# Batch 0's scores computed with tokens on partitions, and x of the other batches loaded without states

## Chip, cores and metric

One core of one Trainium2 chip. The metric is device time in microseconds of one execution. The kernel before: median 666.43 us of three runs (665.96 to 667.14). Its profiled execution took 665.46 us, 663.3 of them from the first instruction to the last.

## What is computed

For each of 8 batches and 8 heads, 512 tokens `x` and 32 states `state` of 64 numbers attend to each other, and the result, 544 rows of 512 numbers a batch, goes through a gated layer:

```python
scores  = scale * x @ state.T          # 512 x 32, softmax over the states
xread   = softmax(scores)  @ state     # 512 rows out
scores2 = scale * state @ x.T          # 32 x 512, softmax over the tokens
sread   = softmax(scores2) @ x         # 32 rows out
h = concat(xread, sread) reshaped to 4352 x 512
out = ((h @ w_a) * (h @ w_b)) @ w_out  # d_ff = 1536
```

## The kernel before

**Stages.** The program is recorded first and ordered afterwards. `Recorder` (L195 on) collects units: one instruction, or several under `rec.together`. `plan` (L699) works out from given costs when each unit is due (`late`), adds to that the table `SHIFTS` (L316) and gives each unit an earliest time from the table `RELEASES` (L530), both by a running number of groups of units; then it fills the engines' queues in time. Within an engine the order is fixed by this; SP issues all DMAs in one order. All instructions are issued by one loop, so the profile puts nearly all of them down to L1798, and one goes by the tiles' names.

**Order of the work.** `VISITS` (L33) lets each batch pass through the d_ff chunks 0 and 1 of 6 (of 256 columns), then the other chunks are worked batch by batch (`SEVEN`, `FOUR`, L35), at last the 256 state rows. Ahead of a batch's first products stands `attend(b)` (L1617); the weights are brought in and split by `open_chunk` (L1674), `Conv` and `Whole` (L917, L960). TensorE works with pairs of tiles `_h` and `_l`: a number is split into a high part and a rest, and a product is three products of parts.

**Batch 0's way to its first product.** `Attention.load` (L1100) loads x transposed: for a pair of heads, features on 128 partitions (two heads of 64), 512 tokens in the free dimension, two such pairs for each of two groups `g`. The host appends to each of these 512 columns 64 of the states, padded: the first head's 32 states stand in the first 64 rows and 32 columns, the second head's in the other rows and columns, and zeros elsewhere. So a row of x is 576 numbers, `self.x` its first 512 and `self.st` the rest. The tile `x` has one buffer. Of batch 0, group 0 comes in two loads, one for each half `h`; all other groups come in one.

`scores(g)` (L1111) multiplies float32 states (64x32) by x (512 columns), four products for a group, each into 32 rows of a PSUM tile `ms`. So states are on partitions, heads in the order of `place_of` (L992). `copied(g)` (L1128) brings that into one half of `p_raw` on ScalarE, `store` (L1135) writes it to DRAM (`kept`) for the softmax over tokens, which comes in `read(b)` (L1653) much later.

The softmax over states needs states in the free dimension. A batch in `WIDE` (L51), that is batch 0 alone, gets there by TensorE: `scores_t` (L1138) transposes the four blocks of 128 tokens into an `acc` tile (`acc<-ident,p_raw` in the profile). `soft_t` (L1146) takes the maximum over 32 states and subtracts it on VectorE; `exp` (L1192) is ScalarE's; `norm` (L1195) is sum, +1e-9, reciprocal and product on VectorE; `back_t` (L1154) transposes back on TensorE (`acc<-ident,s_p`) and splits the result into high and low part with help of a product by -1 (`parts_of`, L898: `sd_h`, `sd_l` are batch 0's two tiles). The other batches go through `turn` and `back` (L1184, L1204), where VectorE transposes 32x32 blocks itself, and their `scores` are made for both groups at once.

For the first products (`ab<-sd_h,p_h` and the like, `product`, L1419) the weights' share for a batch is made by `direct` (L1298): states on 64 rows from `states_raw` (L1061, tile `xst`, all batches' states, loaded in four pieces), times converted weights `wo`. `states_raw` is loaded for batches 0 to 3 first and for 4 to 7 not before 50 us in the plan's time.

**Filling.** Before there is work, TensorE multiplies a tile `y` by itself, `WARM` = 80 times (L892 to L896), into a tile that nothing reads. The order of these among other units is the plan's.

**The end.** The last state rows leave through `layer2` (L1457): for the last 128 rows the two halves of 256 columns are multiplied, added and stored one after the other, columns 256 to 511 first (L1468).

Of the kernel before, what the change touches and what calls it, by code (L numbers as in the profile page):

```python
# [295 lines left out]
class Engine:  # L296
# [20 lines left out]
    0: 961, 1: 522, 2: -345, 3: -1004, 4: 175, 5: 340, 6: 86993674, 7: 86992534, 8: -40, 9: 377, 10: -272, 11:  # L317
    -285, 12: 1910712395119901894770688, 13: -228, 14: 836668491679242834149376, 15: -10, 16: 1824, 17: -285,
    18: -10666, 20: 605, 21: -1033, 22: 528, 23: 107510836717052703539200, 24: 539, 25: 53223186493590233677824,
    26: -1380, 27: 130, 28: -254, 29: 177, 30: -397, 31: 21675430, 32: -630, 33: 783445305185652701134848, 34:  # L320
    -951, 35: -13, 36: -642, 37: -5155, 38: 36215977, 39: -877, 40: 48965331574103428038656, 41: 42, 42: -635,
    43: -1228, 44: -269, 45: 2071, 46: -472, 47: -577, 48: 102188518067693636550656, 49: -9, 50: 676, 51: 520,
    52: 719217, 53: 33, 54: 714, 55: 53223186493590233677824, 56: -11, 57: 13732, 58: 517, 59: -2841, 60: 177,
    61: -972, 62: -23, 63: -53223186493590208512000, 64: 873, 65: 818137, 66: -164, 67: -474, 68: 604052, 69:
    -208, 70: 817687, 71: 2541, 72: -322, 73: 1208, 74: 707126, 75: -2962, 76: 593704, 77: -285, 78: -413, 79:
    369, 80: 593791, 82: -710700, 83: -27, 84: -173, 85: 110582, 86: -140, 87: 240, 88: 125076, 89: 85, 90:
    1396, 91: 32, 92: 6008, 93: 407, 94: -1248, 95: -79, 96: -1909, 97: -119, 98: 383, 99: -172095, 100: 629,
    101: -276, 102: -439, 103: -61, 104: -8159, 105: -1335, 106: 102, 107: 179, 108: -391, 109: -217, 110: 190,
    111: -26, 112: 6, 113: 64, 114: -1302, 115: 76, 116: 150039, 117: -631, 118: 183174, 119: -7, 120: 611, 121:
    225, 122: -3461, 123: -347, 124: -31117, 125: -316, 126: -250, 127: -119, 128: 662, 129: 197, 130: 291, 131:  # L330
    -53, 132: 476, 133: -1773, 134: 979, 135: 496, 136: -53223186493590208512000, 137: -619, 138: 5, 139: 448,
    140: 161, 141: 208554, 142: -104, 143: 1036873, 144: 784, 145: -43, 146: -759, 147: 635, 148: -24167, 149:
    795, 150: -2348, 152: 18204, 154: -118, 155: 1344, 156: -1474, 157: 78, 158: 2092, 159: -1478, 160: -272,
    161: -418, 162: -31, 163: -417, 164: -25074, 165: -2, 166: 17936, 167: -71, 168: -7661, 169: -270, 170:
    -18782, 171: 213, 172: 216, 173: -1, 174: -716, 175: -1464, 176: 691, 177: -323, 178: -579, 179: -194, 180:
    50, 181: 59, 182: -276, 183: -464, 184: -69, 186: 18395, 187: 122, 188: -49252, 189: 484, 190: 1157, 191:
    1278, 192: -12766, 193: 1667, 194: -127, 195: -358, 196: 3208, 197: 52, 198: 33, 199: -563, 200: -301, 201:
    109, 202: -119779, 203: 119, 204: -25, 205: -454, 206: 20, 207: -5082, 208: -388458, 209: 581, 210: -6, 211:
    -2508, 212: 471, 213: 316, 214: -242, 215: 1314, 216: -1260, 217: -731, 218: 306, 219: 1, 220: -120, 221:
    1068, 222: -8035, 223: -1303, 224: -20681, 225: 925, 226: 38867, 227: -408, 228: -232, 229: -10521, 230:  # L340
    330, 231: -11913, 232: 60, 233: 391, 234: -7142, 236: 3392, 237: -2739, 238: -903, 239: 305, 240: -163, 241:
    -688, 242: 303, 243: -2430, 244: -1182, 245: 137, 246: 104, 247: -610, 248: -102, 249: -208, 250: 196, 251:
    16, 252: 650, 254: -101, 255: -62, 256: 73, 257: -98, 258: 602, 259: 110, 260: 4, 261: 184, 262: -43, 263:
    -114, 264: -270, 265: 379, 266: 2005, 267: -144, 268: 305, 269: 172, 270: 1565, 271: 262, 272: -266, 273:
    1021, 274: 389, 275: 215, 276: 3038, 277: 233, 278: 665, 279: -618, 280: -2599, 281: 2762, 282: -483, 283:
    -652, 284: -429, 285: -17, 286: -7023, 287: -1082, 288: -25, 289: -694, 290: -10, 291: 1559, 292: 2347, 293:
    1599, 294: 145, 295: 347, 296: 700, 297: -436, 298: 555, 299: 1336, 300: -46, 301: 677, 302: 494, 303: -188,
    304: -614, 305: -1829, 306: 332, 307: 178, 308: -480, 309: -933, 310: 131, 311: -747, 312: -496, 313: -423,
    314: 219, 315: -289, 316: -421, 317: 28, 318: 904, 319: -283, 320: -309, 321: -429, 322: -381, 323: 651,
    324: 1261, 325: -662, 326: 12, 327: -714, 328: 132, 329: -520, 330: 718, 331: -1558, 332: 112, 333: -554,  # L350
    334: -354, 335: -772, 336: 429, 337: 112, 338: -755, 339: -867, 340: -2, 341: 654, 342: -385, 343: 2716,
    344: -754, 345: 801, 346: 60, 347: 1152, 348: 1039, 349: 137, 350: 2270, 351: 1354, 352: 296, 353: 226, 354:
# [1488 lines left out]
```

## Time and profile before

| what | value |
|---|---|
| median of three runs | 666.43 us |
| profiled execution, whole | 665.46 us |
| its span, first to last instruction | 663.3 us |
| PE busy | 654.2 us (99%) |
| DVE busy | 548.8 us (83%) |
| ACT busy | 383.0 us (58%) |
| moved by DMA | 155.98 MB, mean 235 GB/s |
| chain that ended last | PE 93%, DVE 5%, issue 1% |

PE is TensorE's products, PEld its weight loads, DVE VectorE, ACT ScalarE, SP the engine whose queue issues the DMAs. A busy PE counts the modelled ends of pipelined products, so that neighbouring ones overlap. A row of the timeline merges neighbours of one kind: `x8` are eight of them, the length is from the start of the first to the end of the last. Names are written out<-in with buffer numbers left out. In square brackets stands the idle time of the engine before the row and what ended it.

### The profile page before, as it was taken

How to read it: one execution, taken by the hardware profiler on the slowest of the kernel's cores; microseconds unless marked ns; L12 is line 12 of the kernel's file. 1: busy time of each engine (PE TensorE's matmuls, PEld its weight loads, DVE VectorE, ACT ScalarE, POOL GpSimd, SP SyncE). 2: the span in 40 equal slices, each digit the busy share in tenths (PEclk: the TensorE clock that was granted, in tenths of full speed). 3: DMA queues.
4: the chain of work that ended last, by engine and by line, in shares of the span. 5: the costliest groups of instructions: out<-in, count | busy, mean ns of one | idle time of the engine just before them, and what ended most of it. 6: DMA issues, size and time to landing. Idle time of an engine off the chain costs nothing.

```text
span 663.3 us, 12126 instructions
## 1 busy us (share of the span) xinstructions
PE 654.2 (99%) x4451; PEld 546.1 (82%) x4451; DVE 548.8 (83%) x1219; ACT 383.0 (58%) x707; POOL 0.7 (0%) x6
## 2 busy tenths in 40 slices
PE   7999999999999999999999999999999999999997
PEld 5566776776777778888888989898989989889996
DVE  5999989998877787878989978877777879877885
ACT  4677478699989976654545543534444444424442
POOL 0000000000000000000000000000000000000000
PEclk9999999999999999999999999999999999999999
DMA  8998579899989999866767764754426217168830
GB/s 304 354 366 332 222 253 344 301 317 356 351 300 393 339 327 351 328 189 198 257 235 219 246 232 124 249 168 159 155 101 169 102 48 223 65 182 188 233 97 33
DMA packets 75450, 155.98 MB, mean 235 GB/s; under 512 B 7040, under 2 KB 26240, under 8 KB 75392
## 3 DMA queue, kind: packets, MB, share of 16 engines
q1 hardware_dynamic: 75392, 155.22, 69.9%
q8 instruction: 35, 0.57, 0.4%
q14 instruction: 23, 0.19, 0.1%
HBM read 92.27 MB, written 62.91 MB: 234 GB/s over the span
## 4 chain that ended last, share of the span: by engine, by line
PE 93%; DVE 5%; issue 1%; DMA 0%; ACT 0%; DVEq 0%
PE ab L1798 44%; PE acc L1798 39%; PE ms L1798 10%; DVE t L1798 1%; DVE wo L1798 1%; DVE m L1798 1%; DVE s_p L1798 1%; DMA x<-xt 0%; DVE stg L1798 0%; DVE p_l L1798 0%; DVE x L1798 0%; ACT p_h L1798 0%; DVE a_sb L1798 0%; DVE u_c L1798 0%; DVE wq L1798 0%
## 5 line engine op out<-in xcount | busy, mean ns | idle before, releaser
L1798 PE MATMUL acc<-wo,g_h 128*128 128x256 f32 (+1 forms) x868 | 178.8, 316 | 0.3 <-DVE stg L1798 0.2
L1798 PEld LDWEIGHTS acc<-wo,g_h 128*128 128x128 f32 x868 | 135.4, 190 | 19.5 <-issue 3.4
L1798 PE MATMUL ab<-at_l,p_h 128*128 128x512 f32 x368 | 144.5, 393 | 0.0
L1798 PE MATMUL ab<-at_h,p_h 128*128 128x512 f32 x368 | 144.4, 397 | 0.0
L1798 PE MATMUL ab<-at_h,p_l 128*128 128x512 f32 x368 | 143.1, 391 | 0.0
L1798 PE MATMUL acc<-wo,g_l 128*128 128x256 f32 (+1 forms) x587 | 127.3, 308 | 0.2
L1798 PEld LDWEIGHTS acc<-wo,g_l 128*128 128x128 f32 x587 | 93.0, 190 | 11.5 <-issue 1.2
L1798 ACT CAST g_h<-a_sb 128x512 fp32r<-128x512 f32 (+1 forms) x104 | 64.0, 615 | 56.3 <-DVE a_sb L1798 26.6
L1798 PEld LDWEIGHTS ab<-at_h,p_h 128*128 128x128 f32 x368 | 69.1, 188 | 17.5 <-issue 2.9
L1798 PEld LDWEIGHTS ab<-at_h,p_l 128*128 128x128 f32 x368 | 69.1, 188 | 15.5 <-issue 0.8
L1798 PEld LDWEIGHTS ab<-at_l,p_h 128*128 128x128 f32 x368 | 69.3, 188 | 12.1 <-issue 0.8
L1798 DVE TENSOR_TENSOR g_h<-a_sb,g_h 128x512 fp32r<-128x512 f32 x68 | 46.7, 686 | 15.6 <-PE acc L1798 11.7
L1798 ACT COPY wq<-ab 128x512 f32<-128x512 f32 (+1 forms) x48 | 27.3, 569 | 43.5 <-PE ab L1798 43.3
L1798 DVE TENSOR_TENSOR wq<-ab,wq 128x512 f32<-128x512 f32 (+1 forms) x48 | 32.0, 666 | 21.9 <-PE ab L1798 18.9
L1798 ACT CAST p_h<-p_raw 128x1024 fp32r<-128x1024 f32 x32 | 33.7, 1054 | 21.7 <-PE ab L1798 20.5
L1798 DVE TENSOR_TENSOR p_l<-p_raw,p_h 128x1024 fp32r<-128x1024 f32 x32 | 39.0, 1218 | 1.5 <-ACT p_h L1798 1.4
L1798 DVE TENSOR_TENSOR stg<-acc,stg 128x256 f32<-128x256 f32 (+1 forms) x68 | 36.4, 552 | 3.6 <-PE acc L1798 2.6
L1798 ACT CAST g_l<-wq 128x384 fp32r<-128x384 f32 x46 | 23.6, 515 | 27.1 <-PE acc L1798 24.4
L1798 DVE TENSOR_TENSOR g_l<-wq,g_l 128x384 fp32r<-128x384 f32 x46 | 25.5, 555 | 14.5 <-PE acc L1798 9.8
L1798 ACT COPY p_raw<-ms 128x512 f32<-128x512 f32 x48 | 27.6, 591 | 10.7 <-PE ms L1798 8.5
L1798 DVE TENSOR_SCALAR t<-t 128x512 int32<-128x512 int32 x64 | 26.8, 420 | 5.3 <-ACT t L1798 5.0
L1798 DVE TENSOR_TENSOR a_sb<-ab,a_sb 128x512 f32<-128x512 f32 (+1 forms) x36 | 23.6, 657 | 6.7 <-PE ab L1798 5.3
(135 smaller groups left out, 1065.3 us busy)
## 6 DMA issues: line engine op xcount, KB each, us to landing
p_raw<-scr SPq DMA_DIRECT2D x32, 512.0 KB, 4.8
raw<-wl SPq DMA_DIRECT2D x20, 512.0 KB, 5.6
x<-xt SPq DMA_DIRECT2D x15, 576.0 KB, 7.1
out<-stg SPq DMA_DIRECT2D x33, 256.0 KB, 2.3
su<-wq SPq DMA_DIRECT2D x16, 512.0 KB, 5.8
scr<-sw_st SPq DMA_DIRECT2D x32, 256.0 KB, 4.6
scr<-p_raw SPq DMA_DIRECT2D x32, 256.0 KB, 4.8
x<-xn SPq DMA_DIRECT2D x16, 512.0 KB, 5.1
```

The source lines that it names most:

```text
L1798: getattr(obj, method)(*map(real, args), **{k: real(x) for k, x in kw.items()})
```

## The change

For batch 0, `scores_t` no longer transposes scores: it computes them again in the layout that it needs. Blocks of 128 tokens of x are the weights (128 rows, both heads), the 64 padded state columns are what is streamed, and the product lands with tokens on partitions. That is eight products a group. In this layout group 1's heads stand in another order than `place_of` has it, so its subtraction is done in two halves that put the columns right. The row scores of batch 0 (states on partitions) are made after that for both groups in one set; their copies and stores follow. The extra cost that the plan adds to the first scores (600) goes over to group 0's `scores_t`.

Batches 1 to 7 take their states for the row scores from `states_raw`, and their x is loaded without the 64 padded columns of each row (512 numbers in two runs for a partition, in place of one run with both rows and paddings). The tile `p_raw` is taken at the scores instead of at the first copy. At the end, the two halves of the last 128 rows change places. Both tables of the plan are replaced as a whole, so the order of instructions on all engines is a new one; of their some 730 changed lines the first of each stand here.

```diff
@@ -314,372 +314,377 @@
 
 
 SHIFTS = {
...
-    0: 961, 1: 522, 2: -345, 3: -1004, 4: 175, 5: 340, 6: 86993674, 7: 86992534, 8: -40, 9: 377, 10: -272, 11:
...
+    1: -301, 2: 282, 3: -635, 4: -579, 5: 1064, 6: 306437818579271978743496704, 8: -142422053665657027033038848,
...
 }
 
 RELEASES = {
...
-    0: 72, 1: 82, 2: 106, 5: 521, 6: 18, 8: 43, 9: 53, 10: 80, 13: 117, 14: 129, 19: 101, 20: 121, 21: 141, 23:
...
+    0: 12, 1: 115, 2: 125, 4: 495, 5: 531, 6: 56, 7: 55, 8: 61, 9: 89, 11: 130, 14: 187, 15: 191, 18: 187, 19:
...
 }
 
 
@@ -1105,29 +1110,28 @@
                     for h in range(2):
                         nc.sync.dma_start(out=x[:, g, h], in_=xt[self.b, g, :, h])
                 else:
-                    u = nc.sync.dma_start(out=x[:, g], in_=xt[self.b, g])
+                    w = S + D if self.wide else S
+                    u = nc.sync.dma_start(out=x[:, g, :, :w], in_=xt[self.b, g, :, :, :w])
                     u.rel = max(0, self.b - 3) * LATER / 2
 
         def scores(self, *gs):
 
             for g in gs:
                 self.s[g] = ps_ms.tile([P, 512], F32, name="ms")
-            with rec.together() as u:
+            self.pair = mlp.tile([P, NG, S], F32, name="p_raw")
+            with rec.together(self.pair) as u:
                 for hq in range(4):
                     for g in gs:
                         hh, j = hq % 2, place_of(g, hq)
                         rows = slice(hh * D, (hh + 1) * D)
                         nc.tensor.matmul(self.s[g][j * NS:(j + 1) * NS],
-                                         lhsT=self.st[rows, g, hq // 2, hh * NS:(hh + 1) * NS],
+                                         lhsT=self.st[rows, g, hq // 2, hh * NS:(hh + 1) * NS] if self.wide else
+                                         states_raw[rows, 2 * g + hq // 2, self.b * NS:(self.b + 1) * NS],
                                          rhs=self.x[rows, g, hq // 2], start=True, stop=True)
             if len(gs) == 1:
                 alone(u)
-            if self.b == 0 and gs == (0,):
-                late(u, 600)
 
         def copied(self, g):
-            if g == 0:
-                self.pair = mlp.tile([P, NG, S], F32, name="p_raw")
             self.e2[g] = self.pair[:, g]
             nc.scalar.copy(out=self.e2[g], in_=self.s[g])
             self.s[g] = self.e2[g]
@@ -1139,9 +1143,14 @@
 
             self.t = psp.tile([P, 512], F32, name=tag)
             self.sp[g] = att.tile([P, 16, 32], F32, name="s_p")
-            with rec.together(self.sp[g]):
+            with rec.together(self.sp[g]) as u:
                 for sb in range(4):
-                    nc.tensor.transpose(self.t[:, sb * P:(sb + 1) * P], self.s[g][:, sb * P:(sb + 1) * P], ident)
+                    x, o = slice(sb * P, (sb + 1) * P), self.t[:, sb * P:(sb + 1) * P]
+                    for h in range(2):
+                        nc.tensor.matmul(o.rearrange("p (i h n) -> p h i n", i=2, h=2)[:, h], lhsT=self.x[:, g, h, x],
+                                         rhs=self.st[:, g, h].rearrange("p (i n) -> p i n", i=2), start=True, stop=True)
+            if g == 0:
+                late(u, 600)
 
         def soft_t(self, g):
 
@@ -1149,7 +1158,12 @@
             sp = self.sp[g]
             t = self.t.rearrange("p (a b) -> p a b", b=32)
             nc.vector.tensor_reduce(out=m1[:, 0, :], in_=t, axis=AX.X, op=ALU.max)
-            minus(nc.vector, sp, t, m1[:, 0, :].unsqueeze(2).broadcast_to([P, 16, 32]))
+            top = m1[:, 0, :].unsqueeze(2).broadcast_to([P, 16, 32])
+            if g == 0:
+                minus(nc.vector, sp, t, top)
+            for i in range(2) if g else ():
+                o, a, b = (v.rearrange("p (s i h) n -> p s i h n", s=4, i=2)[:, :, j] for v, j in ((sp, 1 - i), (t, i), (top, i)))
+                minus(nc.vector, o, a, b)
 
         def back_t(self, g, psp, tag):
             ps = psp.tile([P, 512], F32, name=tag)
@@ -1465,7 +1479,7 @@
             for _ in range(-(-len(fill) // (nt - i))):
                 fill.pop(0)()
             ends = last and final and u is units[SU] and i == nt - 1
-            for x in (slice(DM // 2, DM), slice(0, DM // 2)) if ends else (slice(0, DM),):
+            for x in (slice(0, DM // 2), slice(DM // 2, DM)) if ends else (slice(0, DM),):
                 for k, (l, r) in enumerate(((gh, 0), (gh, 1), (gl, 0))):
                     paced(nc.tensor.matmul, u.acc[i][:, x], dict(lhsT=l[:, ts], rhs=wo[ft][:, r, x],
                                                                  start=(first and k == 0), stop=(last and k == 2),
@@ -1623,18 +1637,15 @@
         where = acc if b == 0 else ms
         if a.wide:
             for g in range(NG):
-                a.scores(g)
-                a.copied(g)
                 a.scores_t(g, *where)
                 a.soft_t(g)
                 a.exp(g)
                 a.norm(g)
                 a.back_t(g, *where)
-                if a.keeps:
-                    a.store(g)
-                else:
-                    a.soft(g)
-                    a.out(g)
+            a.scores(0, 1)
+            for g in range(NG):
+                a.copied(g)
+                a.store(g)
             return
         a.scores(0, 1)
         for g in range(NG):
```

## Rows read from the trace of the kernel before

**Rows 1.** Busy time by stretches; count behind each; clock, DMA share, GB/s.

```profile
0.00:8.15 8.15, 4.50 (x17) 2.24 (x18) 0.00 (x1) 2.18 (x3) 0.71 (x6) 1.00 0.75 228
8.15:25.84 17.69, 16.41 (x138) 12.39 (x137) 17.48 (x38) 9.28 (x17) 0.00 (x0) 1.00 1.01 366
...
37.40:50.00 12.60, 12.59 (x92) 8.72 (x93) 12.43 (x26) 9.22 (x18) 0.00 (x0) 1.00 1.02 402
50.00:75.00 25.00, 25.00 (x159) 18.16 (x158) 24.69 (x52) 17.87 (x34) 0.00 (x0) 1.00 0.76 295
...
sum 663.30, PE 654.17 PEld 546.06 DVE 548.80 ACT 383.03 POOL 0.71; mean PE 93.45 PEld 78.01 DVE 78.40 ACT 54.72 POOL 0.10
```

**Rows 2.** PE's waits, 25.9 us to the end (total, times, longest).

```profile
PE ab L1798 <- ACT p_h L1798: 0.5, 1, 0.5
PE acc L1798 <- DVE stg L1798: 0.2, 1, 0.2
```

**Rows 3.** Chain of waits, 0 to 75 us (start, length, what).

```profile
7.18 0.94 PE acc L1798 x4
...
8.15 0.70 DVE m L1798
...
36.73 0.63 ACT g_h L1798
```

**Rows 4.** Timeline, 0 to 32 us (start, length, what, idle before).

```profile
3.65 2.60 PE L1798 MATMUL ms<-x 64*32 64x512 f32 x8 [3.65 <-DMA x<-xt]
4.33 0.18 PEld L1798 LDWEIGHTS ms<-x 64*32 64x32 f32 x4 [0.50 <-DMA x<-xt]
...
6.29 0.59 ACT L1798 COPY p_raw<-ms 128x512 f32<-128x512 f32 x1 [3.96 <-PE ms L1798]
...
8.56 0.67 ACT L1798 ACTIVATE t<-raw 128x512 f32<-128x512 f32 x1 [1.68 <-DMA raw<-wl]
...
8.87 0.69 DVE L1798 TENSOR_TENSOR s_p<-acc,m 128x512 f32<-128x512 f32 x1
...
9.60 0.63 ACT L1798 ACTIVATE s_p<-s_p 128x512 f32<-128x512 f32 x1 [0.37 <-DVE s_p L1798]
...
11.69 0.81 SPq L1798 DMA_DIRECT2D x<-xt  x2
...
16.79 0.69 DVE L1798 TENSOR_REDUCE m<-acc 128x16 f32<-128x512 f32 x1
...
20.67 0.70 DVE L1798 STREAM_TRANSPOSE s_p<-p_raw 128x512 f32<-128x512 f32 x1
...
22.01 1.28 DVE L1798 TENSOR_TENSOR s_p<-s_p,m 128x512 f32<-128x512 f32 x2
22.04 0.67 ACT L1798 ACTIVATE t<-raw 128x512 f32<-128x512 f32 x1 [0.53 <-DMA raw<-w_out]
...
25.84 0.50 PE L1798 MATMUL ab<-sd_h,p_h 128*128 128x512 f32 x1 [0.47 <-ACT p_h L1798]
```

**Rows 5.** DVE's longest waits, whole span.

```profile
DVE m L1798 <- PE acc L1798: 8.1, 1, 8.1
```

**Rows 6.** Chain of waits, 240 to 330 us: a read.

```profile
276.83 1.03 PE ms L1798 x64
```

**Rows 7.** Tile x up to 25 us (ns min/median/max, first and last start).

```profile
L1798 PE MATMUL ms<-x x32: 586/613/1058, 3.6 to 19.2; 64*32 64x512 f32 x32
```

**Rows 8.** Tile xst up to 60 us (issue ns, first and last start).

```profile
L1798 SPq DMA_DIRECT2D xst<-sd x4: 539/583/657, 7.3 to 49.4; - x4
```

**Rows 9.** Timeline of PE, 40 to 60 us.

```profile
48.72 0.39 PE L1798 MATMUL ab<-at_h,p_h 128*128 128x512 f32 x1
```

**Rows 10.** Timeline, 655 us to the end.

```profile
659.12 0.28 PE L1798 MATMUL acc<-wq,g_l 128*128 128x256 f32 x1
...
659.48 0.28 PE L1798 MATMUL acc<-wq,g_l 128*128 128x256 f32 x1
...
659.79 0.76 DVE L1798 TENSOR_TENSOR stg<-acc,stg 128x256 f32<-128x256 f32 x2 [0.24 <-PE acc L1798]
```

727 rows, old and new, of tables (RELEASES, SHIFTS) are left out of this document.

## Prediction

> **What bounds the kernel now.** First the busy time by stretches [rows 1]. Over the whole span PE is busy 654.17 of 663.3 us and DVE 548.80, but the shares differ: from 37.40 us on PE is full, and of the first 8.15 it is busy 4.50. Up to 25.84 most of what it does are the 80 products of `y` (L895), which feed nothing. Next PE's waits from 25.9 to the end: two, 0.7 us together [rows 2]. Behind the first product of batch 0, at 25.84 [rows 4], nothing holds PE up. The time is that start, plus a fixed amount of PE work, plus 3.5 us from the last product (it ends at 659.76 [rows 10]) to the end of the last store. A change that alters neither PE's later work nor the tail can only move that start.
>
> What sets the start is shown by the chain of waits [rows 3]: x lands, PE scores, at 8.15 the chain passes to DVE, and it stays there until an ACT cast at 36.73 leads back to PE. DVE idles for 8.1 us before its first maximum [rows 5] and after that hardly at all: busy 17.48 of 17.69 us up to 25.84, 12.43 of 12.60 from 37.40 and 24.69 of 25.00 from 50 [rows 1]. Its load there is two softmaxes of batch 0, the conversion of the weights and batch 1's preparation, and batch 1's first product follows at 48.72 [rows 9]. What makes DVE begin sooner, without idling later, moves the whole queue, and PE behind it.
>
> **The change part by part.** *Batch 0, group 0: the chain.* Before, the eight passes of the row scores end at 6.25; an ACT copy of 0.59 starts at 6.29 [rows 4], four transposes take 0.94 of the chain, and the maximum starts at 8.15 [rows 3]. Copy and transposes go. In place of the scores stand eight float32 products of 64 columns, each two passes (as the four row scores are eight in the trace): 16 passes, in the order block, then half. The first product needs x's first half alone (3.65), its neighbour the second, at whose arrival PE went on at 4.33 [rows 4]; 14 passes follow that. No row has a float32 pass of 64 columns on 128 columns of weights. From above: a transposition has such weights and moves 128 columns, and four took 0.94, so 0.235 each; 14 make 3.3, and the maximum starts at 7.65. From below: the later reads push 64 passes of 64 columns through in 1.03 us [rows 6], four side by side, so 0.064 a step; but the first passes run at about half that pace (a pass of the row scores took 1058 ns at most, at the start, and 613 in the median [rows 7], though the granted clock reads 1.00 throughout, its 2.4 GHz level [rows 1]). That is 0.129 a pass, 14 make 1.8, and with some 0.25 until the last result is there (a reading pass lasts 0.22 by itself) the maximum starts at 6.4. A pass is paced by its columns as far as the rows go, so I take this end: **8.15 becomes 6.4, -1.75**. The other end, 7.65, gives -0.5.
>
> The reads load only 32 columns of weights for each pass, so they don't tell whether a load of 128 hides behind 64 columns. The Trainium skill (TensorE: Matmul & The Clock Gate, section "LDWEIGHTS (loading the stationary operand)") gives a weight load a time that goes with its columns alone, 107 ns for 128. This is more than 64 columns take at full pace, and speaks against products as narrow as these. By that rule alone 14 passes are an estimated 1.5 us, and the sum would come out some 0.3 us better than mine; the 16 passes of group 1, at full pace, would be 1.7 us instead of 1.03. No row of before shows it.
>
> *DVE after the first maximum.* Maximum and subtraction are 0.70 and 0.69, so DVE is through near 7.8 and the exponential (ACT, 0.63) ends near 8.45. But the first weights reach ACT at 8.56 only, after a wait of 1.68 for their load, and take ACT 0.67 [rows 4]. Before, DVE had them to convert while it waited for the exponential; now it has nothing from 7.8 to 8.5: +0.7. There is no hole if group 1's x is put ahead of the weights, so that its maximum fills it. The new tables leave either order open, and neither row is nearer: **+0.35**, ends 0 and 0.7.
>
> *Group 1's subtraction* becomes two of 256 columns. Two additions of that width at the end take 0.76 [rows 10], one subtraction of 512 columns 0.69: **+0.07**. Its scores and transposes were ready well before DVE came to their maximum at 16.79 [rows 4], 8.6 us of full DVE behind the first, so that removing them saves nothing.
>
> *The row scores of batch 0* become one set of 16 passes for both groups, eight side by side as for the later batches: two rounds of 0.61 [rows 7], 1.2 us, where group 0 alone took 2.60. They fall among products that feed nothing: 0. Without that cover, behind 25.84, they cost 1.2. ACT's two copies and SP's two stores into `kept` stay in number; group 0's copy leaves the chain. x's one buffer comes free later: before, batch 1's two loads were issued at 11.69, behind group 1's scores [rows 4]; now they follow group 1's narrow passes and the set, some 0.5 to 1.2 us later. What needs them is batch 1's turning on DVE at 20.67, and DVE has other work up to there: 0. Behind the stores and these loads SP's queue holds `w_out`'s weights, for which ACT waited 0.53 at 22.04 [rows 4].
>
> *Shorter loads.* Each x of batches 1 to 7 is 512 KB in place of 576. In the head DMA is full at 366 GB/s [rows 1], so 64 KB are 0.18 us, and batch 1's two loads bring the weights behind them 0.36 sooner. DVE has no wait for these, ACT has: **-0.1**, ends 0 and -0.36. Later PE waits for no load: 0. The states of batches 1 to 7 now come from `states_raw`; its loads are issued from 7.3 on, before batch 1's x at 11.69, and the last at 49.4 [rows 8], where PE is just past batch 1's first product, and only batches 4 to 7 need it. The passes stay as they are: 0.
>
> *The last two halves* change places. The first addition started at 659.79, 0.03 behind the last of all six products, not behind its own three, which ended at 659.40 [rows 10]. If the other order frees it, 0.34 is gained, else nothing. Nothing in the diff takes that wait away, so I count 0.
>
> *The new tables* order every instruction anew. PE's waits behind 25.84 leave 0.7 to gain; what they can lose is a rival below. I count 0.
>
> **Sum:** -1.75 + 0.35 + 0.07 - 0.1 = -1.43. The profiled execution took 665.46 us around its span of 663.3, so it would take 664.03. The median shown is 666.43, 0.97 above that execution: 665.0. A measurement of this kernel can tell about 0.2%, 1.33 us, so this lies just beyond what counts as faster. With the ends of its terms (maximum at 7.65; no hole, or all of it; the tail 0.34 better) the case spans 664.0 to 665.9.
>
> **The rivals.**
>
> *The weights' landing holds the head.* If a pass is nearer 0.2 us and the first weights still reach ACT at 8.56, the exponential and ACT's conversion fall together, and at 9.5 DVE stands about where it stood before. For it: ACT's wait of 1.68 [rows 4], DMA full [rows 1]. Against it: behind the first load DVE always had other work. -0.2: 666.2. Chance 0.2.
>
> *The order also takes batch 1 out of the head.* DVE turns batch 1's first group at 20.67 (0.70, a maximum of about 0.7, and one of the two subtractions and products at 22.01 that take 1.28): 2.0 us ahead of batch 0's last step [rows 4]. Put behind it, PE starts 2.0 earlier still. Against it: it must be done by 48.72 all the same. 663.0. Chance 0.13.
>
> *DVE and PE fall out of step: slower.* From 37.40 to 75 both are full [rows 1], so no DVE instruction there can be displaced for nothing. The place is DVE's queue ahead of batch 1's first product at 48.72 [rows 9]. If PE starts 1.4 sooner, but the turning of batch 2 (2.0 a group, as for batch 1, 4.0 in all) lands in front of batch 1's last steps, PE waits as long: -1.4 + 4.0 = +2.6, 669.0. It decides from the point where DVE ends batch 1's part later than about 47.3. For it: 0.2 us of slack in those 12.6. Against it: the tables order DVE's work by when it is due. Chance 0.1.
>
> *Nothing begins sooner.* The passes stand in PE's order behind products of `y`, or behind the whole of x, and DVE starts at about 8 as before: 666.4. Against it: PE waited for x itself at 3.65. Chance 0.07.
>
> **How the numbers follow.** The sum's case has 0.5, of which 0.33 lie beyond 0.2% and 0.17 within. With the second rival, faster has 0.46; with the first and the last, within 0.2% has 0.44; slower has 0.1. The predicted time is that of the likeliest case, 665.0. The range, 662.9 to 666.8, reaches down to the second rival and up past the first and the last, and leaves out the slower case and what lies beyond the bounds.
>
> **What would show it.** DVE's first maximum at 6.4 (near 7.65: a pass costs what a transposition does); 16 passes of some 0.13 us; a hole of 0 to 0.7 us ahead of the first sum; PE's first product of batch 0 near 24.4 and batch 1's near 47.3; PE's waits behind them still under 1 us; the tail's first addition behind its own products or not. The forecast is wrong if DVE starts sooner and PE's first product does not, or if PE starts sooner and then waits before 50 us.

## The result, and the profile after

The changed kernel takes 671.26 us (median of 4 runs, 670.57 to 671.39) where the kernel before took 666.44 in the same session: ratio 1.0069, 95% interval 1.0052 to 1.0087. It is slower by 4.8 us; the forecast was 665.0, range 662.9 to 666.8. The profiled execution took 671.39, its span is 669.2. The mean granted clock of the four executions is 0.997 (671.39, the profiled one, and 671.38), 0.999 (671.15) and 1.000 (670.57).

Busy time by stretches of the changed kernel (columns as in [rows 1]), with 25.84 to 37.40 in two parts:

```profile
0.00:8.15 8.15, 4.45 (x17) 3.74 (x18) 0.49 (x1) 1.59 (x2) 0.70 (x6) 1.00 0.67 216
8.15:25.84 17.69, 15.64 (x120) 11.88 (x119) 15.40 (x34) 7.54 (x13) 0.00 (x0) 0.98 0.94 311
25.84:30.00 4.16, 4.16 (x43) 3.60 (x42) 3.86 (x8) 2.43 (x6) 0.00 (x0) 0.68 0.96 317
30.00:37.40 7.40, 7.40 (x57) 4.64 (x50) 6.68 (x14) 5.98 (x15) 0.00 (x0) 1.00 1.05 410
37.40:50.00 12.60, 12.60 (x94) 8.83 (x93) 12.22 (x25) 8.51 (x17) 0.00 (x0) 1.00 1.03 412
50.00:75.00 25.00, 25.00 (x159) 18.17 (x158) 24.82 (x51) 18.87 (x36) 0.00 (x0) 1.00 0.68 256
```

DVE (third busy column) begins sooner, and yet from 8.15 to 25.84 it is busy 15.40 us where it was 17.48 [rows 1]; the DMAs move 311 GB/s there instead of 366. The timeline of PE shows what stands in the way:

```profile
3.70 3.92 PE L1809 MATMUL acc<-x 128*128 128x64 f32 x16 [3.70 <-DMA x<-xt]
7.55 2.67 PE L1809 MATMUL ms<-x 64*32 64x512 f32 x16
...
12.87 0.60 PE L1809 MATMUL acc<-ident,s_p 128*128 128x128 f32 x4
13.30 1.90 PE L1809 MATMUL acc<-x 128*128 128x64 f32 x16
...
21.16 1.04 PE L1809 MATMUL ms<-x,xst 64*32 64x512 f32 x2
24.25 1.17 PE L1809 MATMUL ms<-x,xst 64*32 64x512 f32 x14 [2.05 <-DMA x<-xt]
25.35 3.46 PE L1809 MATMUL ab<-y 128*128 128x256 f32 x15
28.65 0.60 PE L1809 MATMUL acc<-ident,s_p 128*128 128x128 f32 x4
...
30.62 0.40 PE L1809 MATMUL ab<-sd_h,p_h 128*128 128x512 f32 x1
```

SP's queue in the same timeline, the loads of batch 1's x:

```profile
15.23 0.56 SPq L1809 DMA_DIRECT2D x<-xt  x1
15.90 0.53 SPq L1809 DMA_DIRECT2D raw<-w_out  x1
16.48 0.56 SPq L1809 DMA_DIRECT2D x<-xt  x1
```

And DVE in it, the rows with a wait from 7 to 27 us:

```profile
7.66 0.69 DVE L1809 TENSOR_REDUCE m<-acc 128x16 f32<-128x512 f32 x1 [7.66 <-PE acc L1809]
...
9.78 0.69 DVE L1809 TENSOR_REDUCE m<-s_p 128x16 f32<-128x512 f32 x1 [0.70 <-ACT s_p L1809]
...
15.24 0.69 DVE L1809 TENSOR_REDUCE m<-acc 128x16 f32<-128x512 f32 x1 [0.40 <-PE acc L1809]
...
26.07 0.71 DVE L1809 STREAM_TRANSPOSE s_p<-p_raw 128x512 f32<-128x512 f32 x1 [1.11 <-ACT p_raw L1809]
```

Read together: group 1's narrow products (13.30 to 15.2) are the last that read x, so batch 1's x is issued at 15.23 and 16.48 instead of 11.69 [rows 4]. PE has batch 1's row scores in its queue ahead of the transposes back; it waits 2.05 us for x at 24.25, and its granted clock falls: 1.00 up to 25 us, 0.50, the 1.2 GHz level, from 26 to 28, and 1.00 again from 29 (in the mean 0.68 from 25.84 to 30). The 15 idle products behind then take 3.46 us, where 15 took 1.95 in the kernel before:

```profile
14.93 1.95 PE L1798 MATMUL ab<-y 128*128 128x256 f32 x15
```

By the one execution with the clock at 1.000 (670.57) the fall explains some 0.8 us of the 4.8. Batch 0's first product starts at 30.62 instead of 25.84, and DVE meanwhile waited for ACT's copy of the same late scores.

Behind 30 us, the waits of PE (total, times, longest), where the kernel before had 0.2 [rows 2]:

```profile
PE acc L1809 <- DVE stg L1809: 1.1, 2, 0.6
PE acc L1809 <- ACT u_c L1809: 0.5, 1, 0.5
PE ms L1809 <- ACT p_raw L1809: 0.2, 1, 0.2
```

One of the two waits for `stg` is in the tail. Timeline of its last rows, answering to [rows 10]:

```profile
664.32 1.23 DVE L1809 TENSOR_TENSOR stg<-acc,stg 128x512 f32<-128x512 f32 x2 [0.76 <-PE acc L1809]
...
664.57 0.40 PE L1809 MATMUL acc<-wq,g_h 128*128 128x256 f32 x2
...
665.60 0.50 PE L1809 MATMUL acc<-wq,g_h 128*128 128x256 f32 x2 [0.52 <-DVE stg L1809]
...
666.26 0.42 DVE L1809 TENSOR_TENSOR stg<-acc,stg 128x256 f32<-128x256 f32 x1 [0.71 <-PE acc L1809]
```

The first half's addition no longer waits for the second half's products: now the second half's products wait for the first half's addition. From the first product of the last halves to the end of the span it is 4.6 us (669.2 - 664.57), before 4.4 (663.3 - 658.89):

```profile
658.89 0.40 PE L1798 MATMUL acc<-wq,g_h 128*128 128x256 f32 x2
```

### The profile page after: what moved, and what is told of

Its sections match the earlier page's. It is cut to its first block, busy times and chain, and to the rows that moved or that the text cites. A ratio compares the mean times of both kernels' runs of the same rounds, so it can differ in the third digit from the quotient of the medians.

```text
span 669.2 us, 12173 instructions
## 1 busy us (share of the span) xinstructions
PE 658.4 (98%) x4475; PEld 551.0 (82%) x4475; DVE 552.3 (83%) x1220; ACT 381.7 (57%) x707; POOL 0.7 (0%) x6
## 4 chain that ended last, share of the span: by engine, by line
PE 73%; DVE 1%; ACT 1%; issue 0%
PE ab L1809 36%; PE acc L1809 32%; PE ms L1809 5%; ACT wq L1809 0%; DVE m L1809 0%; DVE stg L1809 0%; DVE p_l L1809 0%; ACT sw_st L1809 0%; DVE t L1809 0%; ACT u_c L1809 0%; ACT t L1809 0%; DVE s_p L1809 0%; DVE g_l L1809 0%; DVE wq L1809 0%; ACT p_raw L1809 0%
```

## The experiments

One number recurs: the time that DVE was busy in the first 50 us (the sum of the view of busy time by stretches, of the profiled execution). It belongs, like the start of batch 0's first product, to that one execution, whose own time stands beside it; the time behind that is the median of all. "Late order" is the order of the work behind the head, where "old" is that of the kernel before.

| run | late order | DVE busy to 50 us | first product | that execution, us | time, us | ratio to before (95%) |
|---|---|---|---|---|---|---|
| kernel before | old | 41.44 | 25.84 | 665.46 | 666.1 to 666.4 | |
| changed kernel | new | 38.65 | 30.62 | 671.39 | 671.26 | 1.0052 to 1.0087 |
| e1 | replanned | 38.75 | 27.07 | 688.28 | 688.68 | 1.0308 to 1.0345 |
| e2 | new | 39.69 | 28.45 | 669.65 | 669.85 | 1.0037 to 1.0069 |
| e3 | new | 37.81 | 26.32 | 671.96 | 672.62 | 1.0070 to 1.0113 |
| e4 | old | 41.71 | 25.42 | 665.53 | 666.00 | 0.9986 to 1.0004 |
| e5 | old | 38.62 | 27.91 | 668.84 | 668.77 | 1.0024 to 1.0056 |
| e6 | old | 39.82 | 28.83 | 667.33 | 668.84 | 1.0022 to 1.0046 |
| e7 | new | 41.18 | 26.38 | 667.81 | 667.35 | 1.0007 to 1.0028 |
| e8 | new | 38.52 | 28.66 | 671.34 | 671.19 | 1.0049 to 1.0080 |
| e9 | old | 40.87 | 25.68 | 666.85 | 667.79 | 1.0011 to 1.0030 |
| e10 | old | 38.41 | 27.27 | 670.58 | 668.60 | 1.0024 to 1.0052 |
| e11 | old | 40.92 | 26.58 | 666.50 | 666.65 | 0.9995 to 1.0016 |
| e12 | new | 39.46 | 27.53 | 671.25 | 670.18 | 1.0033 to 1.0067 |
| e13 | old | 41.53 | 25.82 | 666.00 | 666.17 | 0.9992 to 1.0010 |
| e14 | old | 41.30 | 25.46 | 667.19 | 666.23 | 0.9990 to 1.0012 |
| e15 | old | 41.54 | 26.07 | 665.63 | 665.61 | 0.9980 to 0.9998 |

Leaving e1 aside, a microsecond that DVE lost before 50 us goes with a microsecond at the end: its busy time and the time of the same execution add up to 706.9 to 709.0 in the old late order and to 709.0 to 710.7 in the new. The first product alone does not order the times (e3). At like DVE time, the new late order is 2.3 to 2.6 us longer (e6 and e2, e5 and the changed kernel). One profile tells DVE's time to about 1 us: with the head in the same order it is 40.92 in e11 and 41.53 in e13, 38.65 in the changed kernel and 39.82 in e6. The times also hold some 2 us outside the span, in the median 2.2 in the kernel before and 1.8 in e6, e10, e11, e13 and e15; by their spans these five stand 0.35 to 0.5 us worse against the kernel before than by their times. The first four runs set the new order of the work, PE's queue in the head above all, against the parts themselves.

**e1: the changed code planned with the tables of the kernel before.**

```diff
...
-        out.append(100.0 * table.get(n, 0))
+        out.append(100.0 * table.get(OLD[n - 9] if 9 <= n < 30 else n + (n >= 30), 0))
...
```

> The changed code with the tables SHIFTS and RELEASES of the kernel before (group numbers put over; the 21 groups of batch 0's attention take the entries of the groups that they replace). Theory A, the queue: the loss comes from the new order alone, in which batch 1's row scores and 15 products of y stand on PE ahead of group 1's transposes back. Then with the old order PE's first product of batch 0 is at 25 to 26 us and the time is 665.5 to 667.0. Theory B, the parts: the narrow passes, the later release of x and its two runs a row cost the time in any order. Then the first product stays at 28 us or later and the time at 669 to 671.5.

Measured 688.68, far outside both forecasts. The head was no better (DVE 38.75), and behind 60 us PE waited for work that came in another order:

```profile
PE ab L1807 <- ACT p_h L1807: 3.2, 2, 2.4
PE ms L1807 <- ACT sw_st L1807: 2.7, 4, 1.1
PE ab L1807 <- ACT a_sb L1807: 2.0, 3, 1.1
PE ms L1807 <- DVE p_l L1807: 1.5, 1, 1.5
```

The tables add to due times that the plan works out from the program itself; with another program the same tables give another order. So this run tells nothing of the parts; e5 puts the question rightly, with the order itself written out.

**e2: the last 15 of the 80 products of `y` left out** (they feed nothing).

```diff
...
+    gone = [i for i in order if rec.units[i] in warm][-15:]
...
-        for i in order:
+        for i in [i for i in order if i not in gone]:
```

> The changed kernel, its order kept, but the last 15 of the 80 products of y, which stand between batch 1's row scores and group 1's transposes back, are left out (they feed nothing). Theory A: these 15 took 3.46 us of PE at half pace, so the transposes back start near 25.4 instead of 28.55 and the first product near 27.5; time 668.0 to 668.7. Theory B: the transposes back wait for something else as well; less than 1 us is gained, 670.3 or more.

The transposes back follow the row scores at once and the first product comes 2.2 us sooner (28.45), but only 1.4 us reach the end, between the two forecasts: as much as DVE gained (39.69 against 38.65, 1.0) within the spread. Part of it is the clock and not the products: e2's profile has no fall of the clock, and with the head of the changed kernel at the granted clock 1.00 the same 15 take 2.06 us and the first product comes at 28.83 (e6, below), so that leaving them out moves it by 0.4 there. PE still waits 1.47 us for batch 1's x.

**e3: batch 1's row scores, and what depends on them, behind batch 0's first product.**

```diff
...
+    order[a:z + 1] = now + then
```

(From batch 1's row scores to batch 0's first product, `then` holds what depends on those scores, `now` the rest.)

> The changed kernel, with batch 1's row scores, and whatever follows from them, moved in the order from ahead of group 1's transposes back to just behind batch 0's first product. Theory A: the transposes back start when VectorE has written their input, 23.3 us, PE does not wait for x ahead of them, its pace does not fall; the first product is near 25.5 and the time 665.5 to 667. Theory B: 669 to 671.5, since x of batch 1 is as late as before.

The first product comes 4.3 us sooner, at 26.32, and the time is 1.4 longer, above both forecasts. DVE's row shows why:

```profile
29.74 0.71 DVE L1820 STREAM_TRANSPOSE s_p<-p_raw 128x512 f32<-128x512 f32 x1 [2.52 <-ACT p_raw L1820]
```

With PE's queue free, DVE stands 2.52 us for ACT's copy of the same scores. PE has these ready at 27.7, but ACT's queue has a conversion ahead of the copy, which waits 2.53 us, up to 28.58, for its weights. So an early start of PE does not bring the end forward where DVE is held in its queue.

**e4: the kernel before, with x of batches 1 to 7 loaded without states.**

```diff
-                    u = nc.sync.dma_start(out=x[:, g], in_=xt[self.b, g])
+                    w = S + D if self.wide else S
+                    u = nc.sync.dma_start(out=x[:, g, :, :w], in_=xt[self.b, g, :, :, :w])
...
-                                         lhsT=self.st[rows, g, hq // 2, hh * NS:(hh + 1) * NS],
+                                         lhsT=self.st[rows, g, hq // 2, hh * NS:(hh + 1) * NS] if self.wide else
+                                         states_raw[rows, 2 * g + hq // 2, self.b * NS:(self.b + 1) * NS],
```

> The kernel before with one part of the change: x of batches 1 to 7 without the padded states, their states from states_raw; tables of before. Theory A: no part of the loss, PE's first product at 25.5 to 26.2, time 665.8 to 667.2. Theory B (loads in two runs of 2 KB a row take longer than one of 4.6 KB, in a head where DMA is full): batch 1's x lands 1 us or more later than at 17.18 and 18.57, and the time is 667.5 or more.

666.00, the time of the kernel before: this part costs nothing, and gains nothing that can be measured.

**e5 to e8: parts, late order and the last readers of x.** In e5, e6 and e7 the order is a written list in place of the plan's result (`order = ORDER`): e5 has the changed code in the old order, e6 the changed kernel's own order up to 70 us of the plan and the old behind, e7 the kernel before with the new order from 400 us on. e8 is the changed kernel with

```diff
...
+    order.remove(narrow)
+    order.insert(order.index(rows) + 1, narrow)
```

> The changed kernel's instructions, issued in the order that the kernel before has, written out as a list in place of the plan's result: group 0's narrow products stand where its row scores stood, group 1's narrow products and right behind them the row-score set stand where group 1's row scores stood, both stores into kept come later with the load behind them, the copy and transposes of batch 0 are gone, and only the last additions have the new order (with the halves swapped). Theory C (what costs in the head is that x's single buffer comes free later, whatever the order): batch 1's x is issued some 2 us after the kernel before had it (about 14 instead of 12.1) because 32 passes stand where 8 stood, but DVE has work meanwhile, so 665.5 to 667.5. Theory T (the parts are fine, the new tables alone cost the time): DVE starts 0.5 sooner and the tail is 0.5 shorter, 665.0 to 665.8. Theory P (the parts themselves cost what the changed kernel lost): about 671.

> The changed kernel up to 70 us of the plan's time exactly as it is; everything behind in the order of the kernel before (last additions as changed). The lag of the PE against its own work grew in the changed kernel by 3.5 us in the head and by some 3 us more from 140 us on. Theory L (the new order costs about 3 us behind the head, by itself): 668.0 to 669.0. Rival (what is lost behind the head is only the consequence of the late head, any order would lose it): 671 as the changed kernel. Second rival (the head's order and the old late order do not fit each other, as in the run with the old tables): over 673.

> The kernel before, up to 400 us of the plan's time as it is, everything behind in the order of the changed kernel (last additions as before). Theory L: the new order costs 2 to 3 us behind 500 us by itself, so 668.3 to 669.3. Rival (the loss there is a consequence of the head): 666.3, as before.

> The changed kernel with one edit: group 1's sixteen narrow passes are issued right behind the row-score set instead of behind group 0's transposes back, so that x's one buffer comes free at about 12.2 us instead of 15.2. Theory C: batch 1's two loads are issued some 3 us sooner (12.3 and 13.5 if SP's queue lets them), land near 18 and 21, the row scores no longer wait, the transposes back of group 1 start near 25.5 instead of 28.6 and the first product near 27.5 instead of 30.6: 668.0 to 669.5. Rival Q (SP's queue, not x, sets when the loads go: the weights ahead of them): issues stay at 15 to 16.5 and the time stays at 671. Rival R (the products that feed nothing hold the transposes back anyway): x lands sooner, but the first product moves by less than 1 us and the time is 670 to 671.

e5: 668.77, between the theories: the parts cost 2.6 us in the old order too. Batch 1's x is issued at 14.56, and ACT's and DVE's timelines show a second hold:

```profile
14.52 1.07 ACT L2054 COPY p_raw<-ms 128x512 f32<-128x512 f32 x2 [2.39 <-PE ms L2054]
15.48 0.69 ACT L2054 ACTIVATE t<-sd_h 128x512 f32<-128x512 f32 x1
```

```profile
16.20 0.43 DVE L2054 TENSOR_SCALAR t<-t 128x512 int32<-128x512 int32 x1 [2.26 <-ACT t L2054]
```

ACT's queue holds the two copies of the row scores, which wait 2.39 for their passes, and behind them the conversion of the weights that DVE needs; in the kernel before it ran at 13.36:

```profile
13.36 0.71 ACT L1798 ACTIVATE t<-sd_h 128x512 f32<-128x512 f32 x1 [0.48 <-DMA sd_h<-wl]
```

e6 and e7: the new late order costs 1.2 us where it is put in behind 400 us alone (666.13, the median of before then, to 667.35; the forecast was 2 to 3), and 2.4 come back where it is taken out from 70 us on (671.26 to 668.84, as forecast). e6's head stands in the same order as the changed kernel's, but in its profiled execution the granted clock did not fall, and DVE was busy 39.82:

```profile
23.93 1.09 PE L2054 MATMUL ms<-x,xst 64*32 64x512 f32 x14 [1.61 <-DMA x<-xt]
24.95 2.06 PE L2054 MATMUL ab<-y 128*128 128x256 f32 x15
```

So the two profiles are better compared behind the first product: from there to the end of the span it is 636.7 us in e6 (665.5 - 28.83) and 638.6 in the changed kernel (669.2 - 30.62), 1.9 us for the late order. PE's waits behind 50 us in e7's profile are 1.4:

```profile
PE acc L2043 <- DVE stg L2043: 0.6, 1, 0.6
PE acc L2043 <- ACT u_c L2043: 0.5, 1, 0.5
PE ab L2043 <- DVE p_l L2043: 0.3, 1, 0.3
```

Against 0.2 before [rows 2], that is its 1.2. Whether the order costs anything between 70 and 400 us stays open.

e8: 671.19, no change of the time. The passes come at 10.45, but there they take 3.67 us instead of 1.90, and x goes at 14.15 and 15.40, one microsecond sooner, not three:

```profile
10.45 3.67 PE L1815 MATMUL acc<-x 128*128 128x64 f32 x16
```

Group 0's transposes back come at 17.13 instead of 12.87, ACT's queue has their cast ahead of a conversion, and DVE stands 2.06 us for that at 18.95. The wait had moved, as in e3. The first product, at 28.66, stands where e6 has it with the clock at 1.00.

**e9 to e12: what holds DVE.** Batch 1's x in two tiles of its own (room that the later sums use), in the old order (e9) and in the new (e12); ACT's two copies one conversion later in the old order (e10); both (e11).

```diff
+            if self.b == 1:
+                pair = [mlp.tile([P, 2, S], F32, name="stg", bufs=4) for _ in range(NG)]
+                self.x = Both(pair)
+                for g in range(NG):
+                    nc.sync.dma_start(out=pair[g], in_=xt[self.b, g, :, :, :S])
+                return
...
```

> The changed parts in the order of the kernel before (as the run with that order), and batch 1's x in two tiles of its own (the room of the later sums), so that its loads need not wait until batch 0's passes have read the one buffer. In the run without this, VectorE was busy 38.62 us up to 50 us against 41.44 before, and stood 2.26 us at 16.20 for a conversion on ScalarE that had been held by the two copies of the row scores (behind their 16 passes at 14.4), and SP stood from 6.9 to 14.56. Theory X (x's one buffer, by which SP's queue stands, is the whole of the loss): VectorE's busy time up to 50 us back near 41 and 666 or below. Theory S (the copies of the row scores in ScalarE's queue are most of it): the wait at 16.2 stays at 2 us or more, VectorE near 39 to 39.5, 667.8 to 668.8.

> The changed parts in the order of the kernel before, with one edit: ScalarE's two copies of batch 0's row scores stand behind the conversion of the third weights instead of ahead of it; x has its one buffer. Theory S: that conversion starts near 12.5 to 13.4 instead of 15.48, VectorE's wait of 2.26 goes, its busy time up to 50 us rises to about 40.5 and the time falls to 666.3 to 667.3. Theory X: the wait only moves on to what SP's standing queue brings late (the weights of w_out, batch 1's x), VectorE stays near 38.6 to 39.2, 668.3 to 669.

> Both edits together. Both theories: nothing of batch 0's row scores holds VectorE any more, busy up to 50 us about 41.5 to 42, the first product at or ahead of 25.8, and with the last additions 0.5 us sooner 664.8 to 666.0. If it stays above 667, the narrow passes or the split subtraction cost something that neither theory has.

> The changed kernel in its own order, written out as a list, with batch 1's x in two tiles of its own as its only edit. Theory X: the waits for x (3.7 and 2.05 us of TensorE, 2.99 of ScalarE, 1.1 of VectorE) go, VectorE's busy time up to 50 us rises from 38.65 to 41 or more, and about 3 of the 5 us that the changed kernel lost come back: 668.0 to 669.0; what is left is the new order's behind the head. Theory S and the products that feed nothing: 15 of them still stand between the row scores of batch 1 and the transposes back, and ScalarE's weights of w_out come behind; less than 1.5 us come back, 669.8 to 671.

Neither theory is whole. e9: with its own room for x DVE gets 2.25 of the lost 2.82 us back (40.87), the wait at 16.20 shrinks to 0.82 and the first product comes at 25.68; the time is 667.79, 1.0 better than e5 (the profiled execution, 666.85, is the shortest of ten). e10: the copies later alone gain nothing that can be measured. The wait at 16.20 is gone, but in the profiled execution (670.58, the longest of ten) DVE stands 1.20 us at 18.95 for the next conversion and 2.03 at 35.51 for one whose weights were issued at 26.52, behind batch 2's x, which waits for the same buffer: theory X's wait that moves on. e11, both: 666.65, not to be told from the kernel before, but short of the 664.8 to 666.0 expected: DVE still stands 0.83 us for ACT at 18.94. e12 comes out on theory S's side, 670.18: in the new order the loads of x go at 13.51 and 15.03 even with their own room, because SP's queue has `w_out`'s weights and the store into `kept` ahead of them, and DVE stands 1.54 us for group 1's passes where it was 0.40. There the one buffer is one of several holds in a row.

**e13 and e14: the tail, and the best form.** e13 is e11 with the last halves as before; e14 is the kernel before with the halves swapped and the last additions in the new order. This is e14's edit; e13 takes the same line the other way.

```diff
...
-            for x in (slice(DM // 2, DM), slice(0, DM // 2)) if ends else (slice(0, DM),):
+            for x in (slice(0, DM // 2), slice(DM // 2, DM)) if ends else (slice(0, DM),):
```

> The changed parts in the order of the kernel before, batch 1's x in its own tiles, ScalarE's copies of the row scores later, and the last two halves and additions as the kernel before has them. Theory W (the first maximum 0.5 us sooner is worth nothing, because the next weights reach ScalarE no sooner; the swap cost 0.3 at the end): 666.0 to 666.6, no different from the kernel before, and VectorE's idle time up to 50 us as long as before, only with another reason. Rival G (the gain of 0.5 reaches the end): 665.3 to 665.8.

> The kernel before in its own order, with the last two halves swapped and the last additions in the new order: nothing else. From the first pass of the last halves to the end of the span the kernel before took 4.39 us, the changed one 4.65. Theory W: 4.6 to 4.75, a wait of about 0.5 us of TensorE for VectorE's addition ahead of the second half, and a time 0.2 to 0.3 longer, 666.3 to 666.7. Rival (the prediction's other end, the first addition no longer waits for the second half's products): 4.05, 665.8.

e14's rows repeat the tail of the changed kernel:

```profile
660.47 0.40 PE L2043 MATMUL acc<-wq,g_h 128*128 128x256 f32 x2
...
661.51 0.51 PE L2043 MATMUL acc<-wq,g_h 128*128 128x256 f32 x2 [0.53 <-DVE stg L2043]
```

4.6 us to the end of its span at 665.1, as in the changed kernel: the swap costs 0.2 us in the rows, less than the time can tell. e13 comes out at 666.17 against 666.12. Its maximum is at 7.72, and DVE keeps most of that 0.43 us up to group 1's maximum (16.38, before 16.79 [rows 4]); then

```profile
18.18 0.43 DVE L2064 TENSOR_SCALAR t<-t 128x512 int32<-128x512 int32 x1 [0.34 <-ACT t L2064]
```

**e15: e13 with ACT's conversion of the fourth weights ahead of its cast of `sd_l`.**

```diff
...
+    order.remove(150)
+    order.insert(order.index(99), 150)
```

> The best form of the changed parts with one edit: ScalarE's conversion of the fourth weights stands ahead of its cast of sd_l instead of behind it. If ScalarE's order held VectorE: no wait at 18, VectorE's row behind the split subtraction at 17.8, batch 0's first product near 25.4 instead of 25.8, 665.5 to 666.0, less than a measurement can tell from the run without the edit, so that the rows decide. If the lead is lost in any case (another transfer, another queue), a wait of 0.3 to 0.5 turns up elsewhere ahead of 24 and the first product stays at 25.8: 666.0 to 666.4.

That wait goes, and the next takes its place, at the turning of batch 1:

```profile
20.72 0.71 DVE L2064 STREAM_TRANSPOSE s_p<-p_raw 128x512 f32<-128x512 f32 x1 [0.38 <-ACT p_raw L2064]
```

In the kernel before this instruction starts at 20.67 [rows 4]. The time is 665.61 with an interval that just leaves out 1, but neither the first product (26.07) nor the span (663.9) is better than before, so the rows don't bear a gain out. By the medians of the spans, 663.8 against 664.1 in the same session, 0.3 of the 0.76 is left; the rest lies outside the span, and no row says why.

## Why the prediction was wrong

*The reading of the head held for losses.* DVE's queue bounds it, and the table shows it better than the chain did: what DVE loses there goes with a like loss at the end. That a gain passes through in the same way no run shows (e13's 0.43 does not reach the first product). "The time is that start, plus a fixed amount of PE work" fails in e3: the start is 0.5 us later than in the kernel before, and from there to the end of the span it is 643.5 us instead of 637.5.

*The first maximum: mis-sized.* "A pass is paced by its columns" is where I chose the wrong end. 16 passes took 3.92, 0.22 each behind the second half of x, and the maximum came at 7.66: the upper end, 7.65, from the transposition's row. The rival's condition, a pass near 0.2, was met. The Trainium skill (TensorE: Matmul & The Clock Gate, section "LDWEIGHTS (loading the stationary operand)") gives a weight load P / 1.2 ns for P columns, an estimated 107 ns for 128: group 1's passes at 13.30 (1.90 for 16, 0.119 each) come near it. The first sixteen and e8's (0.23) take twice that though the granted clock reads 1.00; why is not shown. So the rule was the better guide for a pass at full pace, and the rows of before for the first ones.

*The hole* was 0.70, the upper end of the term. With both upper ends the terms add up to -0.5 + 0.7 + 0.07 - 0.1 = +0.17, which gives 666.6: the 665.9 that the prediction states as its case's upper end leaves the hole out. With these two sizes the head had nothing to gain in the changed kernel's order.

*The step that failed: "what needs them is batch 1's turning on DVE at 20.67, and DVE has other work up to there: 0".* Three things were wrong in it. x came free not 0.5 to 1.2 us later but 3.5. Group 1's narrow products, which I let precede the release, stood behind group 0's transposes back; but that is the smaller part, for without it x still goes 2.5 us later in e8 and 2.9 in e5, where 16 narrow passes and 16 of the row scores (2.23 and 1.09 us) stand for 8 passes (1.06) of the kernel before. The loads then took until 24, past 20.67, and the queues stand in order: behind batch 1's scores PE had batch 0's transposes back, and behind the first load of batch 1's x SP had `w_out`'s weights, for which ACT waited 2.79 us at 21.80. And DVE's other work depended on ACT, whose queue held the copies of the row scores (e5). The row scores were counted as covered, since they fall among products that feed nothing; their passes are, their copies and the buffer that they hold are not. In the old order this is 2.6 us (e5, the tail's 0.2 in it), and x's own room together with the later copies takes it away, as far as the times can tell (e11).

*The new tables*, counted at 0, failed too: 1.2 us behind 400 us by e7, 2.4 from 70 us on by e6. I had named that what the tables can lose is a rival, but gave that rival a place in the head alone.

*The tail* was counted at 0 with 0.34 to gain. "Nothing in the diff takes that wait away" was wrong, and so was the sign: the addition was freed and the products behind it were held, 0.2 us to the bad in the rows.

*x without states* and *the split subtraction* were right: nothing in e4, 0.76 for two in place of 0.69.

*The rivals.* "DVE and PE fall out of step: slower" had the right sign and, at 669.0, the nearest time; its place was wrong: not batch 2's turning ahead of 48.72, but batch 1's x ahead of 26. "The weights' landing" had a time (666.2) that the parts in their best form reach (e13, 666.17), but not its cause: there DVE keeps its lead past the weights and loses it to ACT's conversion (0.34), in e15 to batch 1's scores (0.38).

The loss of the profiled execution is 5.9 us, of the medians 4.8. Of the 5.9, 2.8 are DVE's time in the head, 1.1 PE's waits from 50 us up to the tail, 0.2 the tail: 4.1; for the rest I have no row. Counted at PE it is whole: 4.8 up to the first product (30.62 against 25.84) and 1.1 behind it (638.6 us to the end of the span against 637.5), though e3 forbids taking the first for a price by itself. By runs, the medians divide into 2.7 for the changed kernel's head with the old late order (e6 against its kernel before) and 2.4 for the new late order (the changed kernel against e6). What in the late order costs this, beyond the waits shown, stays open.

## What to carry over

A product that saves a copy and a transposition reads its input later and longer than the one it replaces: before counting the saving, follow who is waiting for that input's buffer, and every queue in which that load and the result's copies stand ahead of others. Where an engine is full, a lead of half a microsecond is only worth what the next input in its queue allows; in e10 and e15 the wait that was taken away uncovered the next within 3 us. And a table of offsets tuned on one program orders another one differently: to compare orders, write the order out.

## What was not expected

Narrow products of 64 columns on 128 columns of weights cost 0.22 us a pass at 3.7 us, 0.23 at 10.45 in e8 and 0.119 at 13.30, with the granted clock at 1.00, its 2.4 GHz level, in all three stretches. The place in the program does not decide it: in e9 the same passes run at the full pace at 10.37.

```profile
10.37 1.89 PE L2064 MATMUL acc<-x 128*128 128x64 f32 x16
```

Swapping two halves of one PSUM tile that share no number turned a wait of DVE for PE into one of PE for DVE (0.52). And 15 idle products took 3.46 us in place of 1.95 behind a wait of 2.05 us, at a granted clock of 0.54 (25.35 to 28.81), but 2.06 behind a wait of 1.61 in e6, at 1.00.
